# A gated mix on one core: q' turned two tiles at a time, q' begun on kept x tiles, and Wr's pieces made in k' and k'^T x

## The chip, the cores and the metric

The kernel runs on one core of a Trainium2 chip. The metric is device time in microseconds (us); the kernel before takes 727.06 us in the median of three runs (726.32 to 727.85). The names of the engines are those of the profile: PE is the matrix engine (TensorE), PEld its load of weights, DVE the vector engine, ACT the scalar engine, POOL is GpSimd, and SP (SyncE) only issues transfers. "L203" is line 203 of the kernel's file.

## The reference

One input `x` of 2048 rows and 576 columns goes through two branches, and a gate for each row mixes them:

```python
g = sigmoid((x * gate_w).sum(-1, keepdims=True))          # one gate per row
q, k, v = split(x @ wqkv)                                  # 32 heads of 18 columns
pq, pk = phi(q), phi(k)                                    # phi(t) = (t + 1 if t > 0 else exp(t)) + 1e-6
kv  = einsum("bhsd,bhse->bhde", pk, v);  z = pk.sum(s)
num = einsum("bhqd,bhde->bhqe", pq, kv)
den = einsum("bhqd,bhd->bhq", pq, z)[..., None] + 1e-6
a   = concat_heads(num / den) @ wo                         # linear attention
b   = dft_seq_re @ (x @ dft_hid_re.T) - dft_seq_im @ (x @ dft_hid_im.T)   # FNet, real part
y   = g * a + (1 - g) * b
```

## The kernel before, in words

**Number form.** Every fp32 operand is split into a high part (`hi_of`, L173, an ACT copy to the reduced type) and a low part (`lo_of`, L183, a DVE subtraction), and each product is made of three passes of PE: high times high, high times low, low times high. 2048 rows are 16 tiles of 128; 576 columns are four chunks of 128 and a rest of 64, and results come in two halves of 288 columns. One tile against one half takes 14 matmuls of 128x288 (L203): 4 chunks x 3 passes, and the rest chunk, which carries high and low side by side, in 2.

**Stages, in order of time.** A head of 5 us. Then k' (the feature map of k) for 16 tiles, to 64.5 us. Then `k'^T x` (L676) in 20 steps of 5 chunks by 4 quarters, to 129 us; inside it stand `kv_step` (L658, L661), which multiplies the result on by Wv, and the sum for z. Then q' (`q_tile`) for 16 tiles, in whose course the matrix M (kv times Wo) is built, moved and split (`build_kv`, `build_m`, `move_m`, `split_m`), to about 191 us. Then the M loop: q' is normalised (`normalise`, L743 on), turned (`transposed`, L779: PE transposes, ACT makes the high part `qs`, DVE the low part), multiplied by M, scaled by the gate (L1165) and stored (`att`), to 262.5 us. Last come two rounds of the DFT, each with a hidden part (L945) and a sequence part (L1100).

**The DFT's fast scheme** makes 7 products out of 8 blocks. Its left side are sums of pieces of x (`Left(k)`, k from 0 to 8): POOL issues loads of `xb` (L383, or L389 for the rest, k = 8), DVE adds (L193), ACT makes the high and DVE the low part, and POOL stores the result (`xm`, L408); the rest's six stores, `xr` (L419), are issued by SP in `store_rest`. Its right side is `right` (three pieces of Wr, k = 0, 1, 2): POOL loads `wb` (L435), DVE adds, ACT makes the high part of the whole piece (128x2016), DVE the low part in two shares (4x288 and 3x288), and POOL stores each share (`wm`, L454). Every load of POOL here is told to begin after the last ACT operation on record at that place (`done[-1]`).

**Who orders the work.** SP, DVE and ACT work in the order in which the code is written, so an instruction that waits holds up all that is behind it on its engine. PE's and POOL's order is set by the scheduler; PE's is written by hand from the sequence part on.

**Memory that is used twice.** The arena is laid out by hand. The buffer of the rest's `Left` lies on `acc[0]` to `acc[6]`, the results of q': the first DVE write to `acc[0]` in q' therefore has to wait until all six `xr` stores have read that buffer. Four slots hold split x tiles (`xs`). The three sums kv hold 3 of PE's 8 banks until `build_kv` reads them, after the tile q_tile(1).

**q_tile(i)** makes 2 x 14 matmuls; ACT takes relu and exp of each half (L365, L366) and DVE adds them up into `acc` (L367). The second half carries two more columns, of which one is the gate's logit: ACT takes exp (L734), DVE adds 1 and takes the reciprocal on 128x1 (L736, L737). Then the next x tile is loaded, and the tile after next is split into high and low.

Of the kernel before, what the change touches and what calls it, by code (L numbers as in the profile page):

```python
# [14 lines left out]
P = 128  # L15
S, D, H, DH = 2048, 576, 32, 18
NT = S // P
# [62 lines left out]

PRODUCTS = {1: (4, 0), 6: (2, 4), 2: (6, 1), 5: (1, 3), 7: (0, 5), 3: (3, 2), 4: (5, 6)}
# [50 lines left out]
def kernel(  # L132
# [109 lines left out]
    acc = [at(ACC_AT + i * D * 4, [P, D], F, "acc") for i in range(NT)]  # L242
# [269 lines left out]
    order += list(range(FT, NT)) + list(range(NT))  # L512
# [77 lines left out]

    for i in range(FT, NT):
        xs = split.pop(0)
        k_half(i, 0, xs)
# [12 lines left out]
        if i < NT - 1:  # L606
            load_next()
# [59 lines left out]
    for c in range(5):  # L667
        ps = [bank(), bank()]
        passes = FULL if c < KC else FULL[:2]
        for q in range(NCU):  # L670
# [13 lines left out]
            if step in (1, 2):  # L684
                split_next(lo_later)
# [28 lines left out]
            if step >= 12:  # L714
                next(wq_splits, None)
            step += 1
# [8 lines left out]
    def q_tile(i):  # L725
        xs = split.pop(0)
        if i == 0:
            split_next()
        for h in range(2):
            ps = bank()[:, :QH[h]]  # L730
            run(ps, steps(xs, lambda j: wqt.row(h, j)))
            g = gate[:, i:i + 1]
# [3 lines left out]
        nc.vector.tensor_scalar(g, g, 1.0, None, op0=ALU.add)  # L736
        nc.vector.reciprocal(out=g, in_=g)  # L737
# [4 lines left out]
    pz_ring = Ring(T_AT + 40960, D * 4, 4)  # L742

    def normalise(k):
# [10 lines left out]
        for i in range(2):  # L755
# [4 lines left out]
            twices.append(at(T_AT + 36864 + (2 * k + i) % 8 * 512, [P, 2, REST], F, "twice"))  # L760
            rest = acc[2 * k + i][:, KC * P:]
            nc.vector.tensor_copy(out=twices[-1],
                                  in_=rest.unsqueeze(1).to_broadcast([P, 2, REST]))
            yield

    twices = []
# [3 lines left out]
    qs_ring = Ring(T_AT + 50176, XS, 2)  # L770

    def transposed(i):

        xs, _ = new_xs("qs", qs_ring)
        banks = [bank(), bank()]
        twice = twices.pop(0)
        for c in range(5):
            a = acc[i][:, c * P:(c + 1) * P] if c < KC else twice.rearrange("p a b -> p (a b)")
            nc.tensor.transpose(banks[c // KC][:, (c % KC) * P:(c % KC + 1) * P], a, ident)  # L779
        hi_of(xs[:, 0:4], banks[0])  # L780
        lo_of(xs[:, 5:9], banks[0], xs[:, 0:4])
        hi_of(xs[:, 4], banks[1][:, :P])
        lo_of(xs[:, 9], banks[1][:, :P], xs[:, 4])
        return xs
# [7 lines left out]
    mrest = at(T_AT + 32256, [P, D], F, "mraw")  # L792

# [41 lines left out]
    def split_m(h):  # L835
        hi_of(mhi[:, :KC, half(h)], mraw[:, :, half(h)])
        lo_of(mlo[:, :, half(h)], mraw[:, :, half(h)], mhi[:, :KC, half(h)])
        hi_of(mhi[:, KC, half(h)], mrest[:, half(h)])
        lo_of(mhi[64:, KC, half(h)], mrest[64:, half(h)], mhi[64:, KC, half(h)])

    def m_row(h, j):
        return mhi[:, j, half(h)] if j <= KC else mlo[:, j - 5, half(h)]
# [13 lines left out]
    next(norms)  # L856
    q_tile(3)
    go(wr_pieces[0])
    next(norms)
    build_m((0, 1))  # L860
    for i in range(4, NT):
        q_tile(i)
# [3 lines left out]
        for k, j, n in ((0, 4, 2), (0, 5, 1), (0, 6, 2), (1, 4, 1), (1, 7, 2), (1, 8, 1),  # L866
                        (1, 11, 2), (2, 9, 1), (2, 13, 2), (2, 14, 1)):
            if i == j:
                go(wr_pieces[k], n)
        if i in (5, 8, 11, 12, 13):  # L870
            go(norms)
# [456 lines left out]
```

## Time and profile before

| what | value |
|---|---|
| median of three runs | 727.06 us (726.32 to 727.85) |
| profiled execution, its own time | 726.95 us |
| span of the profile | 725.2 us |
| PE busy | 720.0 us |
| DVE busy | 600.5 us |
| ACT busy | 335.7 us |
| POOL busy | 57.1 us |
| mean rate of the DMA engines | 219 GB/s |
| granted TensorE clock | 1.00 in every stage |

The profiled execution stands 0.11 us under the median of the runs. Its own time is 1.75 us longer than the span, which begins with the first instruction and ends with the last. A row of the time line gives the start, the duration and the engine of a group of like instructions that follow each other, its line, its operation, what it writes from what, shapes and count; in brackets stands how long the engine was idle before it and what released it. A row of the chain of waits gives start, duration and what the end of the program hung on in that stretch. Matmuls overlap in their pipeline: one is recorded with a duration that is longer than the distance from one to the next, so PE's time is read from start to start.

### The profile page before, as it was taken

Reading aid. Unit: us, or ns where it says so; the run is one execution under the profiler, and the core shown is the slowest. Engines: PE = TensorE matmul, PEld = TensorE weight load, DVE = VectorE, ACT = ScalarE, POOL = GpSimd, SP = SyncE. Lnnn points to the kernel's source line nnn. Section 1 sums busy time; section 2 is a strip of 40 time slices with the busy share of each in tenths; the row PEclk is TensorE's granted clock in tenths of the full one; section 3 lists DMA queues with packets and bytes.
Section 4 is the critical chain, followed back from the end, with each engine's and each line's share of the span. In section 5 each row is a group of like instructions: output and inputs, shape, how many; then the busy total and the mean of one; then the engine's idle time right before and its main releaser. Section 6 shows DMA issues by size and latency. Waiting matters only on the chain.

```text
span 725.2 us, 13882 instructions
## 1 busy us (share of the span) xinstructions
PE 720.0 (99%) x5444; PEld 718.8 (99%) x5444; DVE 600.5 (83%) x995; ACT 335.7 (46%) x522; POOL 57.1 (8%) x98
## 2 busy tenths in 40 slices
PE   9999999999999999999999999999999999999998
PEld 9999999999999999999999999999999999999997
DVE  5789867589999948989999989767889988788884
ACT  5998346588644444453344334323535332232231
POOL 1011300051032110000000000000000000000000
PEclk9999999999999999999999999999999999999999
DMA  7376795676477999744475675889963543444440
GB/s 256 90 275 221 265 341 176 239 219 231 149 238 285 338 324 379 236 154 139 163 246 176 226 242 179 295 294 396 380 228 129 174 146 136 159 147 150 153 153 33
DMA packets 54372, 158.82 MB, mean 219 GB/s; under 512 B 6436, under 2 KB 11108, under 8 KB 53284
## 3 DMA queue, kind: packets, MB, share of 16 engines
q1 hardware_dynamic: 45060, 118.90, 47.9%
q0 software_dynamic: 8960, 38.65, 14.6%
q8 instruction: 43, 0.70, 0.4%
q10 hardware_dynamic: 288, 0.39, 0.1%
q14 instruction: 21, 0.17, 0.1%
HBM read 115.05 MB, written 41.39 MB: 216 GB/s over the span
## 4 chain that ended last, share of the span: by engine, by line
PE 93%; DMA 3%; DVE 2%; issue 1%; POOL 0%; ACT 0%; SPq 0%; DVEq 0%; ACTq 0%; POOLq 0%
PE bank L1100 48%; PE bank L203 23%; PE bank L945 14%; PE bank L676 3%; PE bank L520 2%; PE bank L779 1%; DMA craw<-in_xg_dram 1%; DMA wraw<-in_wv_dram 1%; DMA xm<-xb 1%; DVE ys L193 1%; PE bank L229 1%; POOL xb L389 0%; PE bank L658 0%; DVE c L183 0%; ACT xb L173 0%
## 5 line engine op out<-in xcount | busy, mean ns | idle before, releaser
L1100 PE MATMUL bank<-fh,c 128*128 128x288 f32 x1792 | 355.1, 294 | 0.3 <-DVE c L183 0.3
L1100 PEld LDWEIGHTS bank<-fh,c 128*128 128x128 f32 x1792 | 286.8, 188 | 0.5 <-DVE c L183 0.5
L1100 PE MATMUL bank<-fl,c 128*128 128x288 f32 x896 | 263.6, 294 | 0.0
L173 ACT ACTIVATE c<-craw 128x1792 fp32r<-128x1792 f32 (+1 forms) x84 | 121.5, 1449 | 187.5 <-DVE craw L193 169.2
L1100 PEld LDWEIGHTS bank<-fl,c 128*128 128x128 f32 x896 | 168.7, 188 | 0.0
L183 DVE TENSOR_TENSOR c<-craw,c 128x1792 fp32r<-128x1792 f32 (+4 forms) x86 | 142.0, 1654 | 6.2 <-ACT c L173 6.1
L193 DVE TENSOR_TENSOR craw<-craw 128x256 f32<-128x256 f32 (+1 forms) x192 | 98.3, 512 | 23.9 <-DMA craw<-in_ci_dram 11.7
L203 PE MATMUL bank<-wd,xs 128*128 128x288 f32 (+1 forms) x784 | 105.9, 296 | 0.0
L203 PEld LDWEIGHTS bank<-wd,xs 128*128 128x128 f32 x784 | 104.6, 188 | 0.1
L945 PE MATMUL bank<-wf,xf 128*128 128x288 f32 x588 | 91.1, 295 | 0.0
L945 PEld LDWEIGHTS bank<-wf,xf 128*128 128x128 f32 x588 | 83.5, 189 | 0.0
L203 PE MATMUL bank<-mw,qs 128*128 128x288 f32 x448 | 63.2, 297 | 0.0
L676 PE MATMUL bank<-pk,c 128*128 128x288 f32 x448 | 61.2, 296 | 0.1
L676 PEld LDWEIGHTS bank<-pk,c 128*128 128x128 f32 x448 | 59.9, 189 | 0.5 <-ACT c L173 0.4
L203 PEld LDWEIGHTS bank<-mw,qs 128*128 128x128 f32 x448 | 59.9, 188 | 0.2 <-DVE qs L183 0.2
L367 DVE SCALAR_TENSOR_TENSOR acc<-bank,e 128x288 f32<-128x288 f32 x64 | 28.1, 453 | 19.8 <-ACT e L366 19.1
L193 DVE TENSOR_TENSOR ys<-bank,ys 128x288 f32<-128x288 f32 x63 | 28.8, 457 | 15.1 <-PE bank L1100 12.0
L183 DVE TENSOR_TENSOR fl<-fl,fh 128x864 fp32r<-128x864 f32 (+1 forms) x32 | 34.6, 1093 | 6.6 <-ACT fh L173 5.3
L173 ACT ACTIVATE fh<-fl 128x864 fp32r<-128x864 f32 (+1 forms) x32 | 29.9, 951 | 16.6 <-DVE fl L193 15.0
L945 PE MATMUL bank<-wf,xr 96*128 96x288 f32 x112 | 33.3, 298 | 0.0
L1165 ACT ACTIVATE acc<-bank,gate 128x288 f32<-128x288 f32 x32 | 16.1, 502 | 35.0 <-PE bank L203 34.8
L193 DVE TENSOR_TENSOR ys<-ys,bank 128x288 f32<-128x288 f32 x47 | 21.2, 450 | 12.3 <-PE bank L1100 11.8
(107 smaller groups left out, 664.9 us busy)
## 6 DMA issues: line engine op xcount, KB each, us to landing
xf<-xm SPq DMA_DIRECT2D x42, 512.0 KB, 9.0
craw<-in_cr_dram SPq DMA_DIRECT2D x32, 512.0 KB, 3.9
craw<-in_ci_dram SPq DMA_DIRECT2D x32, 512.0 KB, 3.4
xraw<-in_xa_dram SPq DMA_DIRECT2D x28, 320.0 KB, 3.5
xm<-xb POOLq DMA_DIRECT2D x8, 1024.0 KB, 6.8
wf<-wm SPq DMA_DIRECT2D x14, 576.0 KB, 5.8
xr<-xr SPq DMA_DIRECT2D x14, 448.0 KB, 8.0
xm<-xb POOLq DMA_DIRECT2D x8, 768.0 KB, 6.4
```

What stands on the lines that cost most here:

```text
L173: return nc.scalar.activation(dst, src, AF.Copy, bias=bias)
L183: nc.vector.tensor_tensor(out=dst, in0=src, in1=hi, op=ALU.subtract)
L193: nc.vector.tensor_tensor(out=dst, in0=a, in1=b, op=op)
L203: nc.tensor.matmul(ps, a, b, start=(n == 0), stop=(n == len(pairs) - 1))
L229: nc.tensor.matmul(warm[:, :P], ones_f, ones_f, start=True, stop=True)
L367: nc.vector.scalar_tensor_tensor(dst, ps, 0.0, e, op0=ALU.max, op1=ALU.add)
L520: nc.tensor.matmul(ps[i][h], x[:, i * P:(i + 1) * P], wkt.row(h, j), start=(c == 0 and n == 0), stop=(c == KC and n == 1))
L676: nc.tensor.matmul(ps[h][:, :HALF], t[:, a, k], pk[s][:, b, half(h)], start=(s == 0 and n == 0), stop=(s == NT - 1 and n == len(passes) - 1))
L779: nc.tensor.transpose(banks[c // KC][:, (c % KC) * P:(c % KC + 1) * P], a, ident)
L945: nc.tensor.matmul(ps, a, b, start=(start and n == 0), stop=(n == len(ops) - 1), skip_group_check=True)
L1100: nc.tensor.matmul(ps[q], c[x][:, l, k], factors[p](y, f), start=(p == 0 and i == 0), stop=(p == NP - 1 and i == 2))
L1165: done.append(nc.scalar.activation(acc[i][:, half(h)], ps[:, :HALF], AF.Copy, scale=gate[:, i:i + 1]))
```

## The change

There are four parts.

1. **Two tiles are turned at once.** `transposed(k)` now turns the four full chunks of both tiles of a pair (8 transposes) and the rests of both, 64 columns each, side by side in one more (`lasts`, copied once for each pair; before, `twice` was copied for each tile and held one rest two times). Each tile's `qs` keeps the high part of its rest on 64 partitions and the low part on the other 64, and the low part of M's rest rows becomes a tile of its own (`mlast`). The matmuls stay 28 for each tile. PE's order is written by hand from the M loop on.
2. **q' begins with kept x tiles.** The tiles 12, 13 and 14 were split for k' and are kept (`kept`); q' takes them first and the others behind (`TURNED`). Three loads of x and three splits fall away.
3. **One gate operation for all tiles.** The 16 pairs of add and reciprocal on 128x1 become one pair on 128x16 ahead of the M loop.
4. **Wr's pieces and the left sums move.** Piece 1 of Wr is made in k', piece 0 in the last steps of k'^T x (its last low share and store behind q_tile(0)), piece 2 wholly in q'; before, pieces 0 and 1 were made in q' and piece 2 from q' into the M loop. `Left(7)` is made in q' and no more in the M loop; ten parts of `normalise` instead of seven stand ahead of the M loop; one load of the hidden part, `load_pair(2)`, is issued at tile 3 of the M loop instead of tile 11. POOL's order follows.

The order of the instructions shows this at three places. On DVE, at the seam of k'^T x and q', before (names with a number are buffers: `plain` are pieces of Wo and Wv, `gt` the results of k'^T x, `xs` the split x tiles, `wb` a piece of Wr):

```order
L183 TENSOR_TENSOR gt_1719<-bank,gt_1719 128x288 x2
L183 TENSOR_TENSOR xs_919<-xraw_920,xs_919 128x640
L367 SCALAR_TENSOR_TENSOR acc_87<-bank,e_1759 128x288
L367 SCALAR_TENSOR_TENSOR acc_87<-bank,e_1779 128x288
L736 TENSOR_SCALAR gate_84<-gate_84 128x1
L737 RECIPROCAL gate_84<-gate_84 128x1
L183 TENSOR_TENSOR plain_1695<-wraw_1696,plain_1695 126x576
L183 TENSOR_TENSOR plain_1716<-wraw_1717,plain_1716 72x576
L367 SCALAR_TENSOR_TENSOR acc_88<-bank,e_1817 128x288
L367 SCALAR_TENSOR_TENSOR acc_88<-bank,e_1837 128x288
```

And the same place after:

```order
L185 TENSOR_TENSOR wb_1525<-wb_1525 128x4x288
L185 TENSOR_TENSOR plain_1669<-wraw_1670,plain_1669 126x576
L185 TENSOR_TENSOR gt_1722<-bank,gt_1722 128x288 x2
L370 SCALAR_TENSOR_TENSOR acc_87<-bank,e_1759 128x288
L370 SCALAR_TENSOR_TENSOR acc_87<-bank,e_1779 128x288
L185 TENSOR_TENSOR wb_1525<-wb_1525 128x3x288
L185 TENSOR_TENSOR plain_1695<-wraw_1696,plain_1695 126x576
L185 TENSOR_TENSOR plain_1717<-wraw_1718,plain_1717 72x576
L370 SCALAR_TENSOR_TENSOR acc_87<-bank,e_1817 128x288
L370 SCALAR_TENSOR_TENSOR acc_87<-bank,e_1837 128x288
```

Both low shares of Wr's piece 0 now stand here, the first ahead of `gt`, the second behind the first two `acc`; the gate's pairs and the low part of an x tile are gone. (After, two tiles share one `acc` buffer, so their number is the same.)

On POOL, in k'^T x and early q', before: `xb` are loads of left sums, `xm` their stores (`xm_108` is that of `Left(5)`), `xb_1243` the loads of the rest's `Left`.

```order
L383 DMA xb_1082<-in_xq_dram 128x2x256 x2
L389 DMA xb_1243<-in_xq_dram 128x2x128 x4
L408 DMA xm_108<-xb_872 128x2048
L408 DMA xm_108<-xb_872 128x1536
L408 DMA xm_109<-xb_1083 128x2048
L408 DMA xm_109<-xb_1083 128x1536
L435 DMA wb_1965<-in_wr_dram 128x3x288
```

And after, where `xm_100` is the store of `Left(5)`, `xb_1236` the loads of the rest and `wm_371` the store of Wr's main pieces:

```order
L411 DMA xm_100<-xb_872 128x2048
L411 DMA xm_100<-xb_872 128x1536
L392 DMA xb_1236<-in_xq_dram 128x2x128 x4
L411 DMA xm_101<-xb_1077 128x2048
L411 DMA xm_101<-xb_1077 128x1536
L438 DMA wb_1525<-in_wr_dram 128x3x288
L438 DMA wb_1525<-in_wr_dram 128x288
L457 DMA wm_371<-wb_1525 128x4x576
L457 DMA wm_371<-wb_1525 128x3x576
```

The stores of `Left(5)` have moved ahead of the rest's loads, and the load and both stores of Wr's piece 0 follow directly on those of `Left(6)`, ahead of all moves of M (`mraw`).

On PE, in the M loop, before: the transposes of one tile and the first three of the 28 products behind them (`mw` are M's parts, `qs` the turned q').

```order
L779 MATMUL bank<-ident_62,acc_91 128x128 x4
L779 MATMUL bank<-ident_62,twice_2768 128x128
L203 MATMUL bank<-mw_1727,qs_2770 128x288
L203 MATMUL bank<-mw_1728,qs_2770 128x288
L203 MATMUL bank<-mw_1727,qs_2770 128x288
```

After: the transposes of two tiles and the first products behind them.

```order
L785 MATMUL bank<-ident_62,acc_90 128x128 x8
L786 MATMUL bank<-ident_62,last_2780 128x128
L205 MATMUL bank<-mw_1730,qs_2783 128x288
L205 MATMUL bank<-mw_1731,qs_2783 128x288
L205 MATMUL bank<-mw_1730,qs_2783 128x288 x2
```

Five transposes for each tile have become nine for each two, and between one group of nine and the next stand 56 products instead of 28.

The diff, cut to its core (of the table `early` and of the plan of the M loop, which move parts of the same work, a line or two):

```diff
+KEPT = 3
+TURNED = [(i - KEPT - 1) % NT for i in range(NT)]
...
-    acc = [at(ACC_AT + i * D * 4, [P, D], F, "acc") for i in range(NT)]
+    acc_pairs = [at(ACC_AT + k * XD, [P, 2, D], F, "acc") for k in range(NT // 2)]
+    acc = [t[:, i] for t in acc_pairs for i in range(2)]
...
-    order += list(range(FT, NT)) + list(range(NT))
+    order += list(range(FT, NT)) + TURNED[KEPT:]
...
+    wr_forms, wr_pieces = right(wr, wr_rest, ((0, ACC_AT + 14336), (1, T_AT + 12 * XD),
+                                              (2, T_AT + 76544)))
+    kept = []
     for i in range(FT, NT):
         xs = split.pop(0)
+        if i >= NT - KEPT - 1:
+            kept.append(xs)
...
+        if i in (4, 5, 6, 7, 9, 10):
+            go(wr_pieces[1])
-        if i < NT - 1:
+        if i < NT - FT:
             load_next()
...
             xg_next(lo_later)
-            if step in (1, 2):
-                split_next(lo_later)
...
             if step >= 12:
                 next(wq_splits, None)
+            if step in (13, 16, 17, 18, 19):
+                go(wr_pieces[0])
             step += 1
...
     def q_tile(i):
-        xs = split.pop(0)
-        if i == 0:
-            split_next()
+        xs = kept.pop(0) if i < KEPT else split.pop(0)
         for h in range(2):
             ps = bank()[:, :QH[h]]
             run(ps, steps(xs, lambda j: wqt.row(h, j)))
-            g = gate[:, i:i + 1]
+            g = gate[:, TURNED[i]:TURNED[i] + 1]
...
-        nc.vector.tensor_scalar(g, g, 1.0, None, op0=ALU.add)
-        nc.vector.reciprocal(out=g, in_=g)
         load_next()
...
+    def transposed(k):
+
+        both = [at(qs_ring.next(), [P, 9, P], R, "qs") for _ in range(2)]
+        mains = [bank(), bank()]
+        last = bank()[:, :P]
+        for i in range(2):
+            for c in range(KC):
+                cs = slice(c * P, (c + 1) * P)
+                nc.tensor.transpose(mains[i][:, cs], acc[2 * k + i][:, cs], ident)
+        nc.tensor.transpose(last, lasts.pop(0).rearrange("p a b -> p (a b)"), ident)
+        for i, t in enumerate(both):
+            hi_of(t[:, 0:4], mains[i])
+            lo_of(t[:, 4:8], mains[i], t[:, 0:4])
+        for i, t in enumerate(both):
+            mine, other = ((slice(0, REST), slice(REST, P))[j] for j in (i, 1 - i))
+            hi_of(t[mine, 8], last[mine])
+            lo_of(t[other, 8], last[mine], t[mine, 8])
+        return both
...
     store_rest()
-    wr_forms, wr_pieces = right(wr, wr_rest, ((0, T_AT + 60416), (1, T_AT + 76544),
-                                              (2, T_AT + 60416)))
-    xs_ring.at[3] = T_AT + 105664
+    xs_ring.at[3], xs_ring.n = T_AT + 34560, KEPT
     load_next()
     q_tile(0)
+    go(wr_pieces[0])
     for f in wo_split:
         f()
     kv_step(4)
     q_tile(1)
     build_kv()
     q_tile(2)
...
+    early = {4: [(norms, 2)], 5: [(norms, 1), (wr_pieces[2], 1)],
...
+        if i == 6:
+            seven = Left(NP - 1, T_AT + (NP - 2) * TPAIR, done[-1]).make()
...
+    nc.vector.tensor_scalar(gate, gate, 1.0, None, op0=ALU.add)
+    nc.vector.reciprocal(out=gate, in_=gate)
...
+    paced.enter_context(tc.manual_schedule(engines={mybir.EngineType.PE}))
     for i in range(NT):
-        qs = nxt
-        if i + 1 < NT:
-            nxt = transposed(i + 1)
+        qs, t = queue.pop(0), TURNED[i]
+        if i % 2 and i + 1 < NT:
+            queue += transposed(i // 2 + 1)
         for h in range(2):
             ps = bank()
-            run(ps[:, :HALF], steps(qs, lambda j: m_row(h, j)))
+            run(ps[:, :HALF], m_steps(qs, h))
...
-        if i == 11:
+        if i == 3:
             hidden.load_pair(2)
```

More of the change, by code (lines that the diff above doesn't have):

```diff
@@ L740, in q_tile @@
             split_next()
-    pz_ring = Ring(T_AT + 40960, D * 4, 4)
+    pz_ring = Ring(T_AT + 39680, D * 4, 3)
     def normalise(k):
@@ L792 @@
     mrest = at(T_AT + 32256, [P, D], F, "mraw")
+    mlast = at(T_AT + 32256, [P, D], R, "mw")
     def build_kv():
@@ L1228, in late @@
             second.load_rest(6)
-    paced.enter_context(tc.manual_schedule(engines={mybir.EngineType.PE}))
     first.load_rest(4)
```

77 lines of the change are left out of this document (33 added, 44 removed).

## The prediction

> **What bounds the kernel now.** First I read the chain that ended last by engine, then the busy time by stage, then the rows of the chain that are not PE's.
>
> ```profile
> PE 93%; DMA 3%; DVE 2%; issue 1%; POOL 0%; ACT 0%; SPq 0%; DVEq 0%; ACTq 0%; POOLq 0%
> ```
>
> ```profile
> 20.00:64.50 44.50, 44.50 (x337) 44.50 (x337) 37.07 (x69) 40.55 (x87) 5.20 (x8) 1.00 0.61 208
> 64.50:129.00 64.50, 64.37 (x491) 63.96 (x490) 51.19 (x85) 33.13 (x57) 9.16 (x14) 1.00 0.73 253
> 129.00:199.00 70.00, 70.00 (x531) 69.90 (x530) 57.49 (x136) 52.28 (x127) 14.54 (x24) 1.00 0.62 206
> 199.00:262.50 63.50, 63.49 (x491) 63.26 (x490) 55.96 (x107) 30.04 (x64) 15.65 (x26) 1.00 0.83 291
> ```
>
> The columns are the stretch, its length, then busy time of PE, PEld, DVE, ACT and POOL, the granted clock, the DMA share and GB/s. The stretches are k', k'^T x, q' and most of the M loop. PE is busy all the time at a clock of 1.00, so the time falls only where PE has less to do or stops waiting, and rises only where PE is made to wait. DVE is next: 37.07 of 44.50, 57.49 of 70.00, 55.96 of 63.50 us; in k' ACT has 40.55 of 44.50. These bear a little more work but no long wait. Busy hides short stalls of PE, as its rows overlap, so I take a pitch from the chain and look for stretches that are longer than their count:
>
> ```profile
> 19.86 44.59 PE bank L203 x336
> 134.06 49.30 PE bank L203 x370
> 203.21 0.55 PE bank L779 x5
> ```
>
> A product takes 44.59/336 = 0.1327 us; 370 of them 49.1, and the row has 49.30, so q' has no stall worth the name. A transpose takes 0.55/5 = 0.11 us.
>
> ```profile
> 98.27 14.13 PE L676 MATMUL bank<-pk,c 128*128 128x288 f32 x100
> 112.24 0.28 PE L658 MATMUL bank<-gt,plain 128*126 128x252 f32 x1
> ```
>
> From 98.27 to 112.24 are 13.97 us for 100 products, which need 13.27: PE lost 0.70 us. The chain tells to what:
>
> ```profile
> 90.31 6.72 DMA xm<-xb
> ...
> 97.53 1.66 SPq L311
> ...
> 99.63 0.03 SPq L578
> ...
> 99.72 7.72 DMA craw<-in_xg_dram
> ...
> 107.53 0.64 ACT c L173
> ```
>
> SP's load of Wq (L311) waited for the landing of `Left(5)`'s store, and behind it stood the load of `craw` for PE's step, which then took 7.72 us.
>
> **The change, part by part.**
>
> *Fewer transposes.* 16 x 5 = 80 become 8 x 9 = 72: 8 x 0.11 = **-0.87 us**, all on PE's path. DVE's copies halve, and its low parts of the rests stay 16 with half the partitions; both are off PE's path.
>
> *POOL's order in k'^T x.* Before, POOL issued the four loads of the rest ahead of `Left(5)`'s store:
>
> ```profile
> 85.31 2.17 POOL L389 DMA_DIRECT2D xb<-in_xq_dram  x3 [2.46 <-DVE xb L183]
> 89.75 1.12 POOL L408 DMA_DIRECT2D xm<-xb  x2
> ```
>
> A low part of DVE released POOL at 85.31; after, the stores follow on the low parts, at about 86 (estimate) instead of 89.75. SP goes on 3 us earlier or more, `craw` too, and the stall needs only 0.70. Its bounds are -0.70 and 0 (if the next of SP's waits takes over). I take **-0.65**: 3 us are four times what is needed.
>
> *Kept x tiles.* Three loads of 320 KB leave SP in k', and three high and low parts leave ACT and DVE. They were hidden beside PE, so: 0, and what covers them is PE's 44.50 and 64.37 us. q3 (the fourth q_tile, counted from 0) is still split from a tile loaded behind `store_rest`, as before.
>
> *Wr's piece 1 in k'.* Two loads and two stores on POOL (busy 5.20 of 44.50 us there), four adds, one high part, two low parts.
>
> ```profile
> 30.97 1.42 DVE L489 SCALAR_TENSOR_TENSOR pk<-acc,pk 128x576 fp32r<-128x576 f32 x2
> 32.67 0.82 DVE L183 TENSOR_TENSOR xs<-xraw,xs 128x640 fp32r<-128x640 f32 x1
> ```
>
> ```profile
> wb<-in_wr_dram POOLq DMA_DIRECT2D x2, 432.0 KB, 4.5
> ```
>
> ```profile
> L193 DVE TENSOR_TENSOR wb<-wb 128x288 f32<-128x288 f32 x16 | 7.1, 456 | 0.3
> L173 ACT ACTIVATE wb<-wb 128x2016 fp32r<-128x2016 f32 x4 | 7.5, 1884 | 1.0 <-DVE wb L193 1.0
> L183 DVE TENSOR_TENSOR wb<-wb 128x1152 fp32r<-128x1152 f32 x4 | 5.4, 1352 | 0.0
> L183 DVE TENSOR_TENSOR wb<-wb 128x864 fp32r<-128x864 f32 x4 | 4.2, 1052 | 0.0
> ```
>
> DVE comes to the first adds behind the low parts of `pk`, at 30.97 + 1.42 = 32.39, and they wait for the loads. Behind the adds stands the low part of tile 8, which ended at 33.49 and which PE wants at 19.86 + 114 x 0.1327 = 34.99. That margin is 1.50, the adds take 2 x 0.456 = 0.91, and 0.59 is left for the wait. If the loads are issued at about 28 (estimate: they follow an ACT operation of tile 4), they land at 32.5 to 33.2, and DVE waits 0.1 to 0.8: a stall of 0 to 0.3. ACT's 1.88 us are the same kind of risk. I take **+0.15**, with bounds of 0 and 0.5.
>
> *Wr's piece 0 at the seam of k'^T x and q'.* This decides the case. `store_rest` fills the DMA engines there, and DVE stands until the six stores have landed, because `acc[0]` lies on their source:
>
> ```profile
> 126.06 5.91 SPq L419 DMA_DIRECT2D xr<-xb  x6
> ```
>
> ```profile
> 132.00:134.00 2.00, 2.00 (x20) 2.00 (x19) 0.00 (x0) 0.97 (x5) 0.00 (x0) 1.00 1.03 405
> 134.00:136.00 2.00, 2.00 (x18) 2.00 (x17) 0.00 (x0) 1.24 (x3) 0.00 (x0) 1.00 0.98 294
> 136.00:138.00 2.00, 2.00 (x17) 2.00 (x17) 0.81 (x3) 0.97 (x4) 0.00 (x0) 1.00 0.39 155
> ```
>
> ```profile
> 126.40 1.26 ACT L173 ACTIVATE plain<-wraw 126x576 fp32r<-126x576 f32 x2
> ...
> 131.69 0.45 ACT L366 ACTIVATE e<-e 128x288 f32<-128x288 f32 x1
> ```
>
> ```profile
> 137.19 0.82 DVE L367 SCALAR_TENSOR_TENSOR acc<-bank,e 128x288 f32<-128x288 f32 x2 [5.72 <-ACT e L366]
> 137.93 0.14 DVE L736 TENSOR_SCALAR gate<-gate 128x1 f32<-128x1 f32 x1
> ...
> 138.18 1.42 DVE L183 TENSOR_TENSOR plain<-wraw,plain 126x576 fp32r<-126x576 f32 x2
> ...
> 140.26 0.14 DVE L736 TENSOR_SCALAR gate<-gate 128x1 f32<-128x1 f32 x1
> ...
> 140.51 0.82 DVE L183 TENSOR_TENSOR xs<-xraw,xs 128x640 fp32r<-128x640 f32 x1
> ```
>
> DVE's idle 5.72 us is put down to ACT's `e`, but that ended at 132.14, and DVE began at 137.19, just after the DMA share fell: the release is the landing. From there to the low part of q3's x tile, which ends at 141.33, are 4.14 us of DVE. PE begins q3 at 134.06 + 56 x 0.1327 = 141.49 and wants that low part behind four products, at 142.02: a margin of 0.69 us.
>
> After, DVE's way there loses two gate pairs (each 138.18 - 137.93 = 0.25, so -0.50) and gains the low share 3x288 (1.05, or 0.97 by pitch): +0.47, which the margin still bears with 0.22 to spare. But the first share is stored by POOL in the full stretch. ACT's high part (1.88) comes about where ACT was done with `plain` at 127.66, so it ends near 129.2; the low share (1.35) ends near 130.5, and the store follows at once. It has 1152 KB:
>
> ```profile
> wm<-wb POOLq DMA_DIRECT2D x4, 1152.0 KB, 6.3
> ```
>
> That is 1.18 MB, at 0.40 MB/us 2.9 us of all DMA engines. While it starts, SP's queue still has at least what the three windows moved: 0.81 + 0.59 + 0.31 = 1.7 MB. If the two queues share, all of the store's 2.9 us lie ahead of the last `xr` landing, less what the x tile's load behind the stores leaves (0.33 MB, a part of it): bounds of 0 and 2.95, and I take 2.7, near the upper end, since the row of `craw` above shows such sharing: 7.72 us while `xm` stores of POOL were under way, where its median is this:
>
> ```profile
> craw<-in_xg_dram SPq DMA_DIRECT2D x20, 256.0 KB, 3.8
> ```
>
> The Trainium skill, "DMA: Bandwidth & Descriptors", section "Queues, rings and completion order", says that a DMA engine goes round the queues that have work, packet by packet; by that rule the store takes its turns at once, and the sum is the one that I take, while if older transfers went first it would be that of the first rival. No row of before has POOL's store inside `store_rest`, so the trace only bears this out by `craw`.
>
> The stall of PE at q3 is then 2.7 + 0.47 - 0.69 = **+2.5 us**, between 0 and 2.8. Queued behind the waiting `acc` on DVE are the splits of Wo, q3's low part and kv's masks; PE's banks wait for it too, but no longer than q3 does. Behind q3 the chain over kv shifts as far as PE does.
>
> *Gate on 128x16.* Off PE's path but for the two pairs counted above. *Piece 2 and `Left(7)` in q', norms earlier.* In q', DVE loses two whole pieces of Wr and 16 gate pairs and gains less, so its 57.49 of 70.00 us falls or stays: 0. *`load_pair(2)` on SP at tile 3 of the M loop* brings 8 tiles of time more for its landing: 0. *The M loop's DVE.* Two tiles' low parts now come in one group. Before, the groups stood here:
>
> ```profile
> 202.44 0.89 DVE L183 TENSOR_TENSOR qs<-bank,qs 128x512 fp32r<-128x512 f32 x2
> ...
> 210.58 0.88 DVE L183 TENSOR_TENSOR qs<-bank,qs 128x512 fp32r<-128x512 f32 x2
> ...
> 218.87 0.89 DVE L183 TENSOR_TENSOR qs<-bank,qs 128x512 fp32r<-128x512 f32 x2
> ```
>
> Two tiles cost DVE 8.14 and 8.29 us; after, PE takes 56 x 0.1327 + 9 x 0.11 = 8.42 us for them, and DVE saves a copy. It keeps up, with little to spare: 0, with an upper bound of 1.
>
> Sum: -0.87 - 0.65 + 0.15 + 2.5 = +1.1 us. The profiled execution of 726.95 becomes 728.1; against the median of 727.06 that is +1.0.
>
> **The rivals.**
>
> *First: the store does not delay `xr` (faster).* If older transfers are served first, or the store starts after about 134, the landing moves by less than 0.22 us, which is the point from which it decides. Then -0.87 - 0.70 to -0.65 and at most +0.15: 725.5. For it: the share falls from 136 on, so a late store finds room. Against it: the DVE order places the share ahead of `gt`, and `gt` may not be late.
>
> *Second: a second wait (slower).* The landing takes the full 2.95 us, DVE then carries its backlog of some 3 us through q', and in the M loop its 8.1 to 8.3 us for two tiles against PE's 8.42 give it nothing back; k' costs 0.5. That is 2.8 + 0.5 + 1 - 1.5 = +2.8, about 729.8. For it: DVE's share in all four stages. Against it: after q3 PE waited for nothing in q' before, and q' frees DVE of two pieces.
>
> *Third: the stall of k'^T x stays*, because SP's next wait takes its place: +0.65 on the forecast, 728.7.
>
> **How the numbers follow.** A change of 0.2%, 1.45 us, is about what a measurement of this kernel can tell from none: under 725.6 is faster, over 728.5 slower. The forecast with its stall of 0.8 to 2.8 us (726.4 to 728.4) and the third rival stand together: 0.35 and 0.12. The first rival has 0.28, of which 0.24 lie under 725.6; the second 0.25. Slower: 0.25 + 0.12 + 0.05 of the forecast's upper end = 0.42; same 0.34; faster 0.24. The predicted time is the forecast's 728.1; the range reaches to the first and second rivals, 725.3 to 730.0. The likeliest's own is 726.4 to 728.7.
>
> **What would show it.** Eight fewer L779-like transposes, 9 in a row at 0.11 each. From the two `kv_step`s in k'^T x, 13.3 us for 100 products and no DMA row of `xm` in the chain near 90 to 107. DVE's first `acc` of q' at about 139.8 instead of 137.19, the `xr` stores landing later, and PE waiting near 142 for `xs`, some 2.5 us. In k', PE short of 44.50 busy by up to 0.3 near 35. I am wrong if DVE's first `acc` begins near 137, if the `wm` store is issued after the `xr` have landed, or if PE waits in the M loop for `qs`.

## The result

The changed kernel takes 733.13 us in the median of six runs (732.01 to 735.0), the kernel before 727.45 us in six runs beside it: a ratio of 1.0081, with a 95% interval of 1.0063 to 1.0098. It is slower by 5.7 us, where 1.0 was forecast and the range ended at 730.0. A second series of the same kernel (a2_after_again below) gave 732.5 us, a ratio of 1.0063 (1.0044 to 1.0081).

The first profile fell on the slowest of these runs, 735.0 us; the one of the second series has 733.0. I take the stages from the second and the single waits from the first, where they are longer but of the same kind. These are the rows of PE's time line in which a stage begins (k'^T x, q', the hidden part, the sequence part), of the kernel before:

```profile
64.29 6.01 PE L676 MATMUL bank<-pk,c 128*128 128x288 f32 x44
...
129.20 3.90 PE L203 MATMUL bank<-wd,xs 128*128 128x288 f32 x28
...
262.37 0.96 PE L945 MATMUL bank<-wf,xb 128*128 128x288 f32 x6
...
314.39 0.30 PE L1100 MATMUL bank<-fh,c 128*128 128x288 f32 x1
```

And of the changed kernel's second series:

```profile
65.97 0.68 PE L686 MATMUL bank<-pk,c 128*128 128x288 f32 x4
...
132.42 3.75 PE L205 MATMUL bank<-wd,xs 128*128 128x288 f32 x27
...
267.62 0.96 PE L965 MATMUL bank<-wf,xb 128*128 128x288 f32 x6
...
320.14 0.30 PE L1120 MATMUL bank<-fh,c 128*128 128x288 f32 x1
```

| stage | before | after | forecast |
|---|---|---|---|
| up to k'^T x | 64.29 | 65.97 (+1.68) | +0.15 |
| k'^T x | 64.91 | 66.45 (+1.54) | -0.65 |
| q' and M loop | 133.17 | 135.20 (+2.03) | -0.87 + 2.5 |
| hidden part | 52.02 | 52.52 (+0.50) | 0 |
| sum | | +5.75 | +1.1 |

Every stage is longer, and the loss has no single cause. Not all of the 1.68 belongs to the change: 0.73 of it had arisen by the first product of L205 (20.43 us, where L203 of the kernel before begins at 19.70), and there the other kernels whose k' is that of before (b1, b2, e7, n1, t1) also differ, from 19.85 to 20.25. From that product to k'^T x are 45.54 us against 44.59, and 46.23 in the first profile. What PE waited for, by the list of PE's waits in the first profile (the engine and line waited for, us in total, times, the longest):

```profile
PE bank L205 <- DVE xs L185: 1.9, 2, 1.4
PE bank L965 <- DMA wf<-wm: 1.8, 1, 1.8
...
PE bank L205 <- DVE acc L370: 1.1, 2, 0.6
PE bank L686 <- DVE c L185: 0.7, 2, 0.4
PE bank L686 <- ACT c L175: 0.7, 1, 0.7
```

The row of `xs` stands for two places, k' (1.4) and the start of q'. The time lines of the changed kernel's first profile show what was late at each place. In k', DVE stands at the adds of Wr's piece 1, and at the stage's end ACT stands before the high part of `pk` 12, which lies on that piece's buffer:

```profile
28.22 1.35 POOL L438 DMA_DIRECT2D wb<-in_wr_dram  x2 [14.84 <-ACT e L368]
...
34.84 0.95 DVE L195 TENSOR_TENSOR wb<-wb 128x288 f32<-128x288 f32 x2 [2.16 <-DMA wb<-in_wr_dram]
...
64.06 0.69 ACT L175 ACTIVATE pk<-acc 128x576 fp32r<-128x576 f32 x1 [4.16 <-DMA wm<-wb]
```

In k'^T x, POOL now issues `Left(5)`'s two stores first, and the third and fourth load of the rest go out late behind them (3.38 and 2.61 us); the last lands when DVE has waited 3.24 us:

```profile
86.78 0.58 POOL L411 DMA_DIRECT2D xm<-xb  x1 [0.79 <-DVE xb L185]
88.16 0.56 POOL L411 DMA_DIRECT2D xm<-xb  x1 [0.79 <-DVE c L185]
89.47 1.45 POOL L392 DMA_DIRECT2D xb<-in_xq_dram  x2 [0.76 <-DVE zacc L195]
94.31 0.74 POOL L392 DMA_DIRECT2D xb<-in_xq_dram  x1 [3.38 <-issue]
97.65 0.72 POOL L392 DMA_DIRECT2D xb<-in_xq_dram  x1 [2.61 <-issue]
...
104.13 1.56 DVE L195 TENSOR_TENSOR xb<-xb 128x256 f32<-128x256 f32 x4 [3.24 <-DMA xb<-in_xq_dram]
```

In the kernel before, DVE came to these adds without a wait:

```profile
97.47 1.55 DVE L193 TENSOR_TENSOR xb<-xb 128x256 f32<-128x256 f32 x4
```

At the start of q', the `wm` store goes out amid the `xr` stores, and DVE waits 7.91 us for their landing:

```profile
134.58 0.77 POOL L457 DMA_DIRECT2D wm<-wb  x1 [18.83 <-DVE wb L185]
...
143.41 0.82 DVE L370 SCALAR_TENSOR_TENSOR acc<-bank,e 128x288 f32<-128x288 f32 x2 [7.91 <-DMA xr<-xb]
```

### The profile page after: what moved, and what is told of

It reads as the page before. It is cut to its first block, busy times and chain, and to the rows that moved or that the text cites. A ratio compares the mean times of both kernels' runs of the same rounds, so it can differ in the third digit from the quotient of the medians.

```text
span 733.2 us, 13795 instructions
## 1 busy us (share of the span) xinstructions
PE 721.9 (98%) x5436; PEld 718.4 (98%) x5436; DVE 593.6 (81%) x954; ACT 333.6 (46%) x519; POOL 57.0 (8%) x98
## 4 chain that ended last, share of the span: by engine, by line
PE 73%; issue 8%; DVE 7%; DMA 6%; ACT 3%; POOL 2%; DVEq 0%; SPq 0%; POOLq 0%; ACTq 0%
PE bank L1120 44%; PE bank L965 13%; PE bank L205 9%; PE bank L686 4%; PE bank L523 2%; DVE c L185 2%; DMA xraw<-in_xa_dram 1%; DVE ys L195 1%; DMA att<-acc 1%; DMA wm<-wb 1%; POOL att L1189 1%; DMA xb<-in_xq_dram 1%; DMA wf<-wm 1%; DMA wb<-in_wr_dram 1%; ACT xb L175 1%
## 5 line engine op out<-in xcount | busy, mean ns | idle before, releaser
L205 PE MATMUL bank<-wd,xs 128*128 128x288 f32 (+1 forms) x784 | 107.1, 296 | 3.0 <-DVE xs L185 1.9
L205 PEld LDWEIGHTS bank<-wd,xs 128*128 128x128 f32 x784 | 104.8, 188 | 4.2 <-DVE xs L185 2.6
L205 PE MATMUL bank<-mw,qs 128*128 128x288 f32 x448 | 61.8, 296 | 0.1
L205 PEld LDWEIGHTS bank<-mw,qs 128*128 128x128 f32 x448 | 59.8, 188 | 0.4 <-DVE qs L185 0.3
L195 DVE TENSOR_TENSOR fl<-bank,y 128x288 f32<-128x288 f32 x48 | 21.6, 451 | 17.6 <-PE bank L965 17.6
L368 ACT ACTIVATE e<-bank 128x288 f32<-128x288 f32 x64 | 25.6, 400 | 12.6 <-PE bank L205 5.8
```

The costliest lines, as they stand in the source:

```text
L195: nc.vector.tensor_tensor(out=dst, in0=a, in1=b, op=op)
L205: nc.tensor.matmul(ps, a, b, start=(n == 0), stop=(n == len(pairs) - 1))
L368: nc.scalar.activation(e, ps, AF.Relu, scale=-1.0)
```

## The experiments

Each difference is against the kernel named in its expectation. The kernel before was run beside each group; its median went from 727.45 to 728.22, so I compare ratios.

**Piece 1 of Wr in k'.** e1 issues the load before the tile loop; e2 also moves the low parts up.

```diff
+    go(wr_pieces[1])
     for i in range(FT, NT):
...
-        if i in (4, 5, 6, 7, 9, 10):
+        if i in (5, 6, 7, 9, 10):       # e1
+        if i in (5, 6, 7, 8, 9):        # e2
```

> The changed kernel, with one edit: the load of Wr's piece 1 in k' is issued before the tile loop of k' instead of behind tile 4; its adds, high and low parts stay where they are. Theory (the adds stand at the head of DVE's queue and wait for a late load): the stall of 1.64 us near 35 us goes, the 0.69 us near 66.6 us stays: 731.5 us against 733.1. Rival (POOL's loads land late wherever they are issued, since the DMA engines are full there): the adds wait as before, 733.1.

> As e1_load_early, and the two low parts and stores of piece 1 one tile earlier (behind tiles 8 and 9 instead of 9 and 10). Theory (the piece lies on the buffers of pk 12 to 15, so ACT's high part of pk 12 waits for the stores to land): ACT's idle time of 4.16 us near 60 to 64 goes, and with it PE's stall of 0.69 us at 66.6: 730.8 us. Rival (that stall comes from DVE's backlog and not from the buffer): it stays, 731.5.

e1: 733.16 us, ratio 1.0072 (1.0057 to 1.0087), no gain that can be told. Yet its mechanism is right: the adds no longer wait, and PE has no gap near 35 us.

```profile
32.70 0.94 DVE L195 TENSOR_TENSOR wb<-wb 128x288 f32<-128x288 f32 x2
```

k'^T x begins 1.4 us sooner than in the first profile of the changed kernel and loses 0.9 of it again: the list of PE's waits of e1 has

```profile
PE bank L687 <- ACT c L175: 1.5, 1, 1.5
```

where it was 0.7. e2: 732.24, ratio 1.0056 (1.0042 to 1.007); ACT's wait of 4.16 us has become 1.50, for another releaser, and PE's gap near 66 is gone. So the late load and the buffer under `pk` 12 were causes, and k' can be mended, but the time hardly follows: the intervals of e1, of e2 and of the two series of the changed kernel overlap.

**The store at the seam.** e3 takes both low parts and stores of piece 0 out of it.

```diff
-            if step in (13, 16, 17, 18, 19):
+            if step in (13, 16, 17, 18):
...
     q_tile(0)
-    go(wr_pieces[0])
...
     q_tile(2)
+    go(wr_pieces[0])
     go(norms, 1)
     q_tile(3)
+    go(wr_pieces[0])
```

> The changed kernel, with the two low parts and stores of Wr's piece 0 taken out of the seam: the first behind q_tile(2), the second behind q_tile(3). Theory (the store shares the DMA engines with the six xr stores and holds up their landing): DVE's first acc of q' comes some 2.7 us earlier against PE's first q' product, and PE's three stalls of 2.4 us between 143 and 148 go: 730.7 us. Rival (the landing is late because of the xr stores and the x tile's load alone, the low share of 3x288 on DVE costs the rest): at most 0.5 us, 732.6.

e3: 730.98 us, ratio 1.0039 (1.0023 to 1.0054). In its time line DVE's first `acc` and PE in q' read:

```profile
132.24 4.54 PE L205 MATMUL bank<-wd,xs 128*128 128x288 f32 x33
137.58 10.75 PE L205 MATMUL bank<-wd,xs 128*128 128x288 f32 x79
...
139.59 0.82 DVE L370 SCALAR_TENSOR_TENSOR acc<-bank,e 128x288 f32<-128x288 f32 x2 [5.52 <-DMA xr<-xb]
```

From q's first product to DVE's first `acc` are 139.59 - 132.24 = 7.35 us, in the changed kernel 143.41 - 132.96 = 10.45: the store held the landing up by 3.1 us. PE's products of q1 to q3 now follow each other without a gap. The stage (q' and M loop) shortens by 2.6 us and the ratio falls by 0.24 to 0.42% of the two series. The store's place is shown to be the cause. The trace also tells which of the six `xr` stores was held up. In the first profile of the changed kernel SP issued them here:

```profile
129.91 6.15 SPq L422 DMA_DIRECT2D xr<-xb  x6
```

The `wm` store of 134.58 went out 0.2 us ahead of the sixth, which begins at 134.78 in this row. By the semaphore updates in the trace, the first five landed 3.6 to 6.2 us after their issue, in e3 3.7 to 6.0; the sixth landed after 8.55 us, in e3 after 5.42. So only the transfer that was issued behind the `wm` store lost time, and it lost all of the 3.1 us.

**The order on POOL.** e4 makes the rest's `Left` a step earlier; e6 lays `acc` out as single tiles; e7 lays it out as pairs in the kernel before.

```diff
-            for k, j, o in ((6, 2, SLOT_AT + 15104), (NP, 6, ACC_AT)):
+            for k, j, o in ((6, 2, SLOT_AT + 15104), (NP, 5, ACC_AT)):     # e4
...
-    acc_pairs = [at(ACC_AT + k * XD, [P, 2, D], F, "acc") for k in range(NT // 2)]
-    acc = [t[:, i] for t in acc_pairs for i in range(2)]
+    acc = [at(ACC_AT + i * D * 4, [P, D], F, "acc") for i in range(NT)]    # e6; e7 the other way round
...
-            if i == 1:
+            if i == 0:
                 lasts.append(at(last_ring.next(), [P, 2, REST], F, "last"))
-                nc.vector.tensor_copy(out=lasts[-1], in_=acc_pairs[k][:, :, KC * P:])
+            nc.vector.tensor_copy(out=lasts[-1][:, i], in_=acc[2 * k + i][:, KC * P:])
```

> The changed kernel, with the rest's Left made at step 5 of k'^T x instead of step 6, by which POOL issues its four loads ahead of Left(5)'s stores again, as in the kernel before. Theory (the loads wait in POOL's queue behind 1792 KB of stores, land at 104 and stop DVE): the stalls of 0.95, 0.28 and 0.57 us between 101 and 110 go and the 0.7 us of the kernel before comes back: 732.0 us. Rival (the DMA engines are full from 91 to 110 whatever the order): the stalls only move, 733.1.

> The changed kernel, with acc as 16 tiles of their own again instead of 8 pairs, and each pair's rests copied to lasts in two copies of 64 columns. By the order of the instructions POOL then issues the four loads of the rest ahead of Left(5)'s stores again. Theory (a pair counts as one tile, so the loads, which lie on acc 0 to 6, wait for the sum over acc 7 too, fall behind 1792 KB of stores and land some 6 us later): the first adds of the rest wait no more near 104, the stalls of 1.8 us between 101 and 110 go, and the 0.7 us of the kernel before comes back: 732.0 us against 733.1. Rival (the DMA engines are full from 91 to 110 either way): the stalls only move, 733.1.

> The kernel before, with acc laid out as 8 pairs and nothing else; by the order of the instructions this alone puts Left(5)'s stores ahead of the rest's loads. Theory (the new order costs, as the loads wait behind the stores): DVE waits for the rest near 100 to 104 and PE stalls 1.1 us more than before in k'^T x: 728.2 us. Rival, the prediction's term (the stores land earlier and PE's 0.70 us goes): 726.4 us.

e4: 737.65 us, ratio 1.0129 (1.0112 to 1.0146), worse, and by an effect of the edit itself: the sum over `acc` 7 now stood behind the loads and waited for them. PE then waited 4.3 us in one piece, and behind that the granted clock was 0.50 from 100 to 102 us.

```profile
95.89 0.76 DVE L195 TENSOR_TENSOR zacc<-zacc,acc 128x576 f32<-128x576 f32 x1 [7.57 <-DMA xb<-in_xq_dram]
```

The loads lie on `acc` 0 to 6 only. `acc` 7 waits because it shares a pair, and so a dependency, with `acc` 6. That explains the new order on POOL: in the changed kernel the loads have to wait for the sum over `acc` 7 (the releaser `zacc` in the row of 89.47 above). e7 confirms it from the other side: pairs alone, put into the kernel before, give that order and those waits.

```profile
88.52 1.47 POOL L390 DMA_DIRECT2D xb<-in_xq_dram  x2 [0.75 <-DVE xb L193]
92.36 0.72 POOL L390 DMA_DIRECT2D xb<-in_xq_dram  x1 [2.37 <-issue]
95.19 0.72 POOL L390 DMA_DIRECT2D xb<-in_xq_dram  x1 [2.11 <-issue]
...
101.52 1.55 DVE L193 TENSOR_TENSOR xb<-xb 128x256 f32<-128x256 f32 x4 [3.41 <-DMA xb<-in_xq_dram]
```

e7: 729.02 us, ratio 1.0016 (1.0001 to 1.0031): slightly slower, where the prediction's term said faster. Its profile, of an execution of 727.33 us, has 65.51 us for k'^T x where the kernel before has 64.91, so it shows 0.60 of the 1.54 us that the changed kernel loses there. e6: 732.94, ratio 1.0066 (1.0054 to 1.0078). In e6 k'^T x takes 65.7 us instead of 66.5 to 66.7 and the hidden part has no wait, but its M loop, with one DVE copy more for each pair, is 1.1 us longer, and the median hardly moves.

**Part 1 alone.** b1 puts the paired transposes into the kernel before (with single tiles and two copies, as in e6; `transposed`, `m_steps`, `mlast` and PE's order as in the changed kernel); n1 also makes ten parts of `normalise` ahead of the M loop.

```diff
-        if i in (5, 8, 11, 12, 13):
+        if i in (4, 5, 6, 8, 11, 12, 14, 15):       # n1
             go(norms)
```

> The kernel before, with part 1 alone: two tiles turned at once, with acc as 16 tiles and two copies of 64 columns for each pair; PE's order by hand from the M loop on. Theory (8 transposes fewer at 0.11 us): 0.87 us less, 726.2 us. Rival (two tiles' low parts in one group come late, PE waits for qs in the M loop as it did near 243 after the change): 0.3 to 0.6 us of it are lost, 726.6.

> As b1_turn_only, with ten parts of normalise ahead of the M loop instead of seven. Theory (a pair's transposes need both its tiles normalised, and with seven parts the second tile of each pair came late): the waits of some 9 us ahead of the transposes go, and what is left of part 1 is 8 x 0.028 = 0.23 us less than before: 727.5 us against 727.7, the same within the measurement. Rival (the prediction's price of 0.87 us): 726.8. Rival (DVE cannot carry the earlier parts in q', PE waits there): over 728.5.

b1: 736.46 us, ratio 1.0116 (1.0102 to 1.0129); n1: 734.92, ratio 1.009 (1.0076 to 1.0104). The lists of PE's waits have, for b1 and then for n1:

```profile
PE bank L779 <- DVE acc L757: 7.2, 7, 3.1
```

```profile
PE bank L203 <- DVE qs L183: 4.9, 4, 3.4
PE bank L955 <- DMA wf<-wm: 3.5, 2, 1.8
```

Both expectations missed on the time. A pair needs both its tiles normalised before it can be turned, and DVE is late. Part of the loss is a lower granted clock: in b1, behind a wait of 3.05 us, 56 products took 9.05 us instead of 7.51, with the clock at 0.50 from 204 to 206 us; n1 shows the same at 210 to 212 and at 282 to 284 us. In the kernel before, DVE also carries Wr's piece 2 and `Left(7)` in the M loop. That part 1 therefore needs part 4's moves is argued: no run made these moves and part 1 alone.

**The price of a transpose.** t1 leaves out the rest's.

```diff
-        banks = [bank(), bank()]
-        twice = twices.pop(0)
-        for c in range(5):
+        banks = [bank()]
+        for c in range(KC):
...
-        hi_of(xs[:, 4], banks[1][:, :P])
-        lo_of(xs[:, 9], banks[1][:, :P], xs[:, 4])
+        hi_of(xs[:, 4], banks[0][:, :P])
+        lo_of(xs[:, 9], banks[0][:, :P], xs[:, 4])
```

> The kernel before, with the transposes of the rest left out: each tile makes its 4 full transposes only, and the rest's high and low parts are taken from the first 128 columns of the same bank, so that part of the result is not computed; 16 transposes fall away, all else stays. The prediction's price (0.11 us for each): 1.76 us less, 725.9 us against 727.7. Price by the distance from start to start (the last transpose ahead of a product costs 0.028 us, the others 0.109): 16 x 0.028 = 0.45 us less, 727.2 us; the time from q' to the hidden part in the profile shortens by 0.45 us and not by 1.76.

t1: 737.53 us, ratio 1.0145 (1.012 to 1.0169): its time tells nothing on the price, since PE waits in its M loop for other things (the list of its waits has 4.0 us for `qs` of DVE); why, I did not pursue. The price can be read from PE's time line, at tiles where PE does not wait. Before, one tile:

```profile
198.79 0.60 PE L779 MATMUL bank<-ident,acc 128*128 128x128 f32 x4
199.22 0.27 PE L779 MATMUL bank<-ident,twice 128*128 128x128 f32 x1
199.25 3.95 PE L203 MATMUL bank<-mw,qs 128*128 128x288 f32 x28
...
203.51 3.95 PE L203 MATMUL bank<-mw,qs 128*128 128x288 f32 x28
```

After, two tiles:

```profile
205.09 1.03 PE L785 MATMUL bank<-ident,acc 128*128 128x128 f32 x8
205.96 0.27 PE L786 MATMUL bank<-ident,last 128*128 128x128 f32 x1
205.99 7.67 PE L205 MATMUL bank<-mw,qs 128*128 128x288 f32 x56
...
214.39 7.67 PE L205 MATMUL bank<-mw,qs 128*128 128x288 f32 x56
```

In t1, one tile with four transposes:

```profile
211.75 3.96 PE L203 MATMUL bank<-mw,qs 128*128 128x288 f32 x28
215.54 0.60 PE L778 MATMUL bank<-ident,acc 128*128 128x128 f32 x4
215.90 4.01 PE L203 MATMUL bank<-mw,qs 128*128 128x288 f32 x28
```

From one first product to the next are 203.51 - 199.25 = 4.26 us before, 8.40 after and 4.15 in t1. Two tiles cost 8.52 before and 8.40 after: a pair saves some 0.11 us, and so does a tile of t1, each with one transpose less. The average over eleven tiles before is 4.257, over six pairs of c3 (below), whose M loop has no wait of PE, 8.407; eight pairs then save 0.86 us, as forecast. The other price, 0.028 us, which the expectations of t1 and n1 take for the last transpose of a group, counts from the first transpose to the first product alone (0.46 us for five, 0.90 for nine). It leaves out the group's other end: from the first of 28 products to the next transpose are 3.79 us, where 28 products need 3.72.

**SP's order in k'^T x.** b2 issues the first load of Wq a step later in the kernel before; e8 merges e2, e3 and e6, and c1 adds b2's edit to it.

```diff
-            if step in (8, 11):
-                wqt.load(step == 8)
+            if step in (9, 11):
+                wqt.load(step == 9)
```

> The kernel before, with the first load of Wq one step later in k'^T x, behind the loads of craw and Wv that stood behind it. Theory (SP's load of Wq waits for Left(5)'s stores to land, and craw waits behind it in SP's order): PE's 0.70 us near 108 goes, 727.0 us against 727.7. Rival (craw is late because the DMA engines are full, not for its place in SP's order): the stall stays, 727.7.

> The changed kernel with the edits of e2_piece1_early, e3_store_late and e6_acc_apart together. Theory (the stalls are separate): 733.1 less 2.3, 2.4 and 1.1 is 727.3 us. Rival (what PE wins in k' it loses again in k'^T x, where the DMA engines are full, as e1_load_early showed): only e3's 2.4 and e2's 0.9 stay, 729.8.

> As e8_all, with the first load of Wq one step later as in b2_wq_later. Theory: the stall of 1.9 us near 109 us goes, 727.6 us against e8's 729.5 and before's 728.2 to 727.7. Rival (the DMA engines are full there): at most half of it goes, 728.5 or more.

b2: 727.33 us, ratio 0.9994 (0.998 to 1.0008), the same within the measurement; in its profile k'^T x takes 64.26 us instead of 64.91 and PE's gap of 0.70 is gone. e8: 729.48, ratio 1.0019 (1.001 to 1.0028). The chain of waits of its profile, of an execution of 731.93 us, shows the old stall, longer:

```profile
91.67 7.11 DMA xm<-xb
...
99.27 1.48 SPq L313
...
100.86 9.11 DMA craw<-in_xg_dram
...
110.05 0.64 ACT c L175
```

Behind the stall PE is slow as well: the granted clock is 0.50 from 112 to 114 us, and 28 products take 5.55 us instead of 3.72.

```profile
110.73 5.71 PE L686 MATMUL bank<-pk,c 128*128 128x288 f32 x28 [1.73 <-ACT c L175]
```

c1: 728.34, ratio 1.0001 (0.9992 to 1.0009): with Wq's load out of the way the stall is gone, and k'^T x falls from 67.95 to 64.38 us. About half of these 3.57 us is e8's lower clock, and the medians are 1.1 us apart. So the place in SP's order was the cause of this stall, in the kernel before and in e8. Whether it also ate e1's gain is open: the wait of 1.5 us in e1 stands at another place, near 101, and no run put b2's edit on it.

**The M loop.** c1 still waits for `qs` there, 0.8 us. c2 and c3 move left sums.

```diff
-        3: [(0, 1)], 4: [(0, 1)], 5: [(0, 1)], 6: [(0, 1)], 7: [(0, 1)], 8: [(1, 1)],
-        9: [(1, 1)], 10: [(1, 1)], 11: [(1, 1)], 12: [(1, 1)],
+        11: [(1, 1)], 12: [(1, 2)], 13: [(1, 1)],                # c2, behind 3 to 8 as before
+        3: [(0, 1)], 5: [(0, 1)], 7: [(0, 1)], 9: [(0, 1)], 11: [(0, 1), (1, 1)],
+        12: [(1, 2)], 13: [(1, 2)],                              # c3
```

> As c1_all_wq, with the left sums of the M loop moved: four of Left(1)'s five parts go from tiles 9 to 12 to tiles 11 to 13, where normalise has ended. Theory (DVE has 9.46 us of work for two tiles where PE has 8.42, so its low parts of qs fall behind and PE waits 0.94 us near 238): the wait goes, the time from the first product with M to the hidden part falls from 71.1 to 70.1 us, 727.3 us, under the kernel before by 0.1%. Rival (the wait comes from the group of two tiles itself, whatever else DVE does): it stays, 728.3.

> As c1_all_wq, with the left sums of the M loop thinned where normalise still runs: Left(0)'s five parts at tiles 3, 5, 7, 9 and 11 instead of 3 to 7, Left(1)'s at 11 to 13 instead of 8 to 12. In c2_all_spread only parts behind the wait were moved, and DVE had no gap from 212 to 241. Theory (DVE's load): between the groups of qs DVE has one part instead of two, the groups come 8.4 to 8.6 us apart, the wait of 0.94 us near 238 goes and the time from the first product with M to the hidden part is 70.0 us instead of 71.1: 727.0 us where the kernel before has 727.9. Rival (the group of two tiles itself): it stays at 70.8 to 71.1, 728.0.

c2: 728.07 us, ratio 1.0004 (0.9992 to 1.0016), the wait unchanged: it stood ahead of the parts that I moved. c3: **726.66 us, ratio 0.9984 (0.9975 to 0.9994)**, faster than both kernels. The groups of `qs` in c2 came 9.2 to 9.4 us apart ahead of the wait, in c3 at the same place, as here, 8.0 to 8.7, and the M loop's wait is gone:

```profile
219.04 1.61 DVE L185 TENSOR_TENSOR qs<-bank,qs 128x512 fp32r<-128x512 f32 x3
...
227.74 1.61 DVE L185 TENSOR_TENSOR qs<-bank,qs 128x512 fp32r<-128x512 f32 x3
...
235.78 1.60 DVE L185 TENSOR_TENSOR qs<-bank,qs 128x512 fp32r<-128x512 f32 x3
```

It was DVE's load.

**The changed kernel once more.**

> The changed kernel once more, unchanged, since its profile fell on the slowest of its runs (735.0 us of 732.0 to 735.0). The waits in k', k'^T x and at the start of q' are of the change and come again within 0.5 us each; the wait of 1.9 us in the hidden part changes from run to run (0.1 to 1.9 us in the other profiles with acc in pairs, none with acc apart), so it is shorter here: 733.1 us, and stage by stage 1.8, 1.8, 2.5 and about 1 us more than the kernel before.

a2: 732.5 us, as told with the result. By stage, the losses of k', k'^T x and q' came again within 0.3 us, though the wait for `xs` near 36 us was 0.69 instead of 1.37; the hidden part lost 0.5 instead of 2.0.

## Why the prediction was wrong

- **What bounds the kernel** was right: in both profiles of the changed kernel the clock stayed at 1.00, and every loss is a wait of PE.
- **-0.87 for the transposes: right**, price and size. A pair of tiles takes 0.11 us less than two single tiles, so eight pairs save 0.86 us. The stage bears it out: without the store at the seam (e3) q' and the M loop take 0.54 us less than before, and without the M loop's waits too (c3) 1.08 less.
- **-0.65 for POOL's order: this step failed, with its sign, and is the largest miss.** I took the new order for one in which the stores go earlier, and did not ask what then stands behind them. The loads of the rest did: the sentence that bounded the term by 0 "if the next of SP's waits takes over" left out POOL's own queue and DVE, which waits for those loads with all that stands behind. k'^T x lost 1.54 us. Pairing `acc` alone gives that order and that wait (e7), and costs 0.60 us there in e7's profile; with `acc` apart the changed kernel's k'^T x is 0.7 to 1.0 us shorter (e6). Some 0.4 to 0.6 us more is lost at the stage's first products, near 66, where DVE's low part of `c` is late; in e2, which mends k', that gap is gone.
- **+0.15 for piece 1 in k': this step failed too; 1.0 to 1.6 us were lost.** The load landed 34.84 - 28.22 = 6.6 us after its first issue, where I had 4.5 to 5.2; that alone is beyond my bound of 0.5 (0.9 to 1.5 us near 35), and e1 shows it. The margin was also 0.16 smaller than I had it: on the time line k's products begin at 19.70, and the 19.86 that I used is the chain's. And I counted the piece's two stores as POOL's work but did not ask what comes next on their buffer: `pk` 12, whose high part ACT holds until they have landed. e2 shows that.
- **+2.5 at the seam: right in place and size, but not in how the engines share.** From q's first product to DVE's first `acc` are 10.45 us, 2.5 more than before (7.99) and 3.1 more than in e3, against 2.7 taken, and q' lost 2.6 us by e3. (The high part of ACT would, by my own figures, end at 127.66 + 1.88 = 129.54 and not near 129.2; the store still fell into the full stretch.) The Trainium skill's rule ("DMA: Bandwidth & Descriptors", section "Queues, rings and completion order": a DMA engine goes round the queues that have work) is not borne out here: the five `xr` stores issued ahead of the `wm` store took at most 0.2 us longer than in e3, and only the sixth, issued behind it, took 3.1 longer. Service in the order of issue would give the same time. The row of `craw` did not tell the two apart either: two loads of Wq stood ahead of it in SP's own queue and landed at 106.35 and 106.78, 0.7 us before it. If transfers are served in the order of issue, the size was in part luck, for it hung on the store going out 0.2 us ahead of the last `xr`; no run issued it later by so little.
- **0 for the M loop and behind: low.** Two pairs of the M loop took 8.73 and 8.57 us instead of 8.41, waiting for `qs`: 0.5 us, within their bound, though a tile of the kernel before had lost 0.25 as well. The hidden part lost 0.5 to 2.0, for a load of `wf` (its operand from Wr), which SP issues only when an `att` store has landed. I had no term for it, and its cause stays open: with `acc` in pairs the hidden part took 52.5 to 54.0 us (the changed kernel twice, e1, e2, e3), but 52.1 in e4 and 52.0 in e7; with `acc` apart 52.0 (e6, e8, b1, c1, c2, c3), but 57.5 in n1, which waits for `wf` in the same way.
- **The rivals**: the second rival had the right side, but as one backlog of DVE with 2.8 us; the loss came instead from separate waits at places that I had priced near nothing.

## What to carry to other kernels

A moved step is priced by three questions: what stands behind each of its transfers on its own queue, what next writes the buffer that its store still reads, and which other transfers run in that stretch. Two tiles put into one tensor share their dependencies, which can turn a queue's order over far away. The price of a small operation is read over a whole period, from one first product to the next; a part of the period misses what the ends cost. Where four waits stand in line, mending one may only lengthen the next: here, of the single mends, only the store's showed in full in the time, while those of k' and of `acc` stayed within the noise. All together, with SP's order and DVE's load set right, brought the kernel from 0.6 to 0.8% over the kernel before to 0.16% under it.

## What was not expected of the hardware

After 1792 KB of stores on POOL's queue, the third and fourth load of 128 KB were issued 2.1 to 3.4 us late, with nothing waited for that the profile shows (the rows marked "issue"). The stores are not the whole reason: ahead of them, too, three of the four loads went out in 2.17 us and the fourth 1.55 us late in the kernel before, 1.96 late in e6 and 2.27 in e8. A transpose took 0.03 us from start to start where it stood ahead of a product and 0.11 ahead of another transpose, and yet each one left out saved 0.11. Behind a wait of PE of 1.7 to 4.3 us the granted clock fell to 0.50 for some 2 us in the profiles of b1, e4, e8 and n1, but not behind one of 1.8 us in the first profile of the changed kernel. And a wait that PE loses in one stage can return in the next: e1 took 1.4 us out of k', its k'^T x grew by 0.9, and its median did not move.
